# Pooled attention with a gated MLP: the decoding, splitting and copying of the first two batches on other engines, a left-over V tile of its own, a new order

## The chip, the core and the metric

The kernel runs on one core of a Trainium2 chip. The metric is the device time of one execution in microseconds (us); the median of three runs is given with the lowest and the highest. Engines: TensorE (PE, with its weight loads PEld), VectorE (DVE), ScalarE (ACT), GpSimd (POOL), and SyncE (SP), which issues nearly all DMAs from one queue, in order.

## The reference

Eight batches, eight heads, 576 positions of 64. Keys and values are averaged over groups of 8 positions (72 remain), attention over these, then a gated MLP with a spatial gate:

```python
k_p = k.reshape(B, H, Sp, pool, D).mean(axis=3)          # Sp = 72
v_p = v.reshape(B, H, Sp, pool, D).mean(axis=3)
attn = softmax(q @ k_p.T / sqrt(D))                      # 576 x 72 a head
x = (attn @ v_p), heads side by side                     # 8 x 576 x 512
h = gelu_tanh(x @ w_in)                                  # 512 -> 1024
u, v = h[..., :512], h[..., 512:]
v_n = (v - mean(v)) / sqrt(var(v) + 1e-6) * g_ln
v_s = einsum('ts,bsd->btd', w_sg, v_n) + b_sg            # 576 x 576
out = x + (u * v_s) @ w_out                              # 512 -> 512
```

`w_in` and `w_out` come as 64-bit floats, all else as 32-bit floats.

## The kernel before

The large products are taken in fp32r, as three matmuls each: an operand is split into a high part (a cast by ScalarE) and a low part (value minus high part, as a rule by GpSimd), and high*high, high*low and low*high are summed in PSUM.

The work is cut into steps, each a Python generator that issues its instructions stage by stage (a `yield` ends a stage). A step has a letter, a number and a batch:

- A, B: load of the keys and the values (`kvraw`, halves 0 and 1). E: load of what is left over, the groups beyond 128 rows of two heads (`left`). C: load of q (four pairs of heads g).
- K0, K1, P0, P1: pooling of keys and values: on TensorE for batches 0 and 1 (16 rows of matmuls against `ident`, a copy out of PSUM), on VectorE later. K2: pooling of the left-over part (`lp`, VectorE), transposes, and the scaled keys `kbd`. P2: the values as weights: `vb` (or `vbh`, `vbl`), and `vl` for the left-over ones.
- Q: q transposed (`qT`). S0 to S3: scores of a pair of heads, their maximum (`nmax`, VectorE), ten exponentials with sums (ScalarE), normalising (`e`, VectorE), the left-over columns (`el`, GpSimd).
- T0 to T3: e transposed (`ah`, low part `al`), through TensorE in batch 0, through DRAM (`tfar`) later. L: the same for the left-over columns (`lt`, `lfar`).
- V0 to V3: attention times values, then `x32` and its high and low part `xhl`, and for the last 64 positions both parts packed (`xta`).
- H0 to H4: x times the v half of w_in by blocks of positions, Gelu, normalising, `vhh` and `vhl`. U0 to U3: the u half, Gelu. W0 to W3: the spatial product, gate, `ghi` and `glo`. O0 to O3: times w_out, plus x. Z: transposing and storing.
- Weights, once: l.. loads, and v0 to v3, u0 to u3, o0 to o3 decode a quarter of the 64-bit weights: a first step on ScalarE (L1340), three on VectorE (L1342 to L1344), two on ScalarE (L1347, L1348), three on GpSimd (L1350 a product, m; L1351 a subtraction, d; L1352 a sum, a) that give `wil` or `wol`. s0 to s4 transpose and split w_sg.

What sets the order is a table written out by hand, `PROLOGUE` and then `PERIOD` for batch after batch: an entry `S1+0` advances step S1 of batch 0 by one stage; entries for batches that don't exist emit nothing. Each engine gets its instructions in the order of the table and keeps it; semaphores do the rest. PSUM has two tiles each for `mps` (H, U, W, most of O, the scores of batch 0, the decoding of v) and for `aps` (everything of the attention), taken in turn.

In batch 0 (`WHOLE`) the left-over values are written by step P2 over a part of the tile `left` (`v32`), and V reads them from there. Step E of batch 1 loads into the same buffer.

Of the kernel before, what the change touches and what calls it, by code (L numbers as in the profile page):

```python
# [8 lines left out]
F32 = mybir.dt.float32  # L9
# [14 lines left out]
lv0 A1+0 E0+0 K1+0 A0+0 v1 v1 K0+0 v0 v0 K1+0 K2+0 C0+0 Q0+0 K0+0 K2+0 K2+0 Q0+0 S0+0 C1+0 S0+0 S0+0 Q1+0 Q1+0 S1+0  # L24
C2+0 S1+0 Q2+0 S1+0 Q2+0 S0+0 S2+0 C3+0 Q3+0 v0 S1+0 S2+0 Q3+0 T0+0 v1 A0+1 B0+0 S2+0 S3+0 S3+0 A1+1 ls0 B1+0 K1+1
T0+0 S0+0 S3+0 P1+0 S1+0 K1+1 P0+0 lv1 K0+1 S2+0 v0 S3+0 v2 v2 v1 v3 v3 S3+0 P2+0 s1 v2 C0+1 S2+0 v2 s1 K0+1 L0+0 L0+0
s3 v3 lu0 T1+0 V0+0 Q0+1 s3 s1 s3 u0 u0 s2 T1+0 V1+0 lo0 V0+0 u0 s4 o0 V1+0 T2+0 o0 T2+0 T3+0 V2+0 s2 lu1 v3 u1 T3+0
V3+0 u0 V2+0 u2 s2 u1 u1 u2 s4 V3+0 B0+1 B1+1 E0+1 s0 K2+1 C1+1 P1+1 s0 P1+1 P0+1 K2+1 P0+1 K2+1 S0+1 u1 V1+0 V2+0 u2
u3 s4 V0+0 o0 o1 Q1+1 S1+1 s0 S0+1 u3 S1+1 S0+1 S1+1 V1+0 S0+1 V3+0 H0+0 C2+1 Q2+1 H2+0 S1+1 S2+1 V2+0 S2+1 C3+1 Q3+1
S3+1 o1 H0+0 lo1 H2+0 P2+1 C1+2 V3+0 V0+0 u3 S2+1 u2 H4+0 S0+1 o0 H0+0 u3 P2+1 U3+0 H2+0 o2 S3+1 H4+0 T0+1 S3+1 S2+1  # L30
o2 H4+0 o2 o1 S1+1 U3+0 S3+1 S2+1 H0+0 S3+1 o2 T0+1 U0+0 C0+2 L0+1 H4+0 H0+0 H0+0 T1+1 H4+0 o1 L0+1 U0+0 H1+0 P2+1
T0+1 H2+0 L0+1 H3+0 A0+2 P2+1 T0+1 H1+0 H2+0 L0+1 E0+2 V0+1 T1+1 T1+1 Q0+2 H2+0 U2+0 H1+0 Q1+2 H4+0 T2+1 K0+2 T1+1
V1+1 T2+1 H3+0 H3+0 L0+1 H1+0 U1+0 U2+0 H3+0 H4+0 H1+0 T2+1 H3+0 H1+0 A1+2 H3+0 T3+1 H4+0 V0+1 W1+0 V1+1 T2+1 V2+1
# [1159 lines left out]
def tile_pooled_attn_gmlp(ctx: ExitStack, tc: tile.TileContext, q, k, v, w_in, g_ln, w_sg, b_sg, w_out, out):  # L1193
# [96 lines left out]
    gcol = const.tile([P, DF2 // P], F32, name="gcol")  # L1290

    st = {}

    def load(o, i, queue=nc.sync):
        queue.dma_start(o, i)  # L1295

# [219 lines left out]
    def step_P(b, i):  # L1516
# [18 lines left out]
        for h in range(2):  # L1535
            nc.scalar.mul((vb[b] if b in WHOLE else vbh)[:, :, D * h:D * h + D], vp, head[:, h:h + 1])  # L1536
# [388 lines left out]
```

## Time and profile before

| | |
|---|---|
| median of 3 runs | 593.61 us (593.04 to 594.01) |
| the profiled execution: its time, its span | 592.2 us, 590.5 us |
| mean granted clock of TensorE | 0.984 |
| busy in the span: PE, PEld, DVE, ACT, POOL | 548.3, 510.5, 444.5, 357.8, 240.1 us |
| share of PE in the span | 93% |
| share in the chain that ended last: PE, DVE, ACT, DMA, SP's queue | 62%, 9%, 8%, 8%, 4% |
| HBM read and written | 49.73 and 20.94 MB |

Busy time of TensorE is the union of its matmuls' modelled times, so a busy TensorE need not be one at its peak. In rows of waits the first name is what waited, the name behind the arrow what ended the wait. Line numbers are those of the kernel before; all matmuls are issued by one helper at L1237, so groups are told apart by their tiles.

### The profile page before, as it was taken

How to read it: one execution, taken by the hardware profiler on the slowest of the kernel's cores; microseconds unless marked ns; L12 is line 12 of the kernel's file. 1: busy time of each engine (PE TensorE's matmuls, PEld its weight loads, DVE VectorE, ACT ScalarE, POOL GpSimd, SP SyncE). 2: the span in 40 equal slices, each digit the busy share in tenths (PEclk: the TensorE clock that was granted, in tenths of full speed). 3: DMA queues.
4: the chain of work that ended last, by engine and by line, in shares of the span. 5: the costliest groups of instructions: out<-in, count | busy, mean ns of one | idle time of the engine just before them, and what ended most of it. 6: DMA issues, size and time to landing. Idle time of an engine off the chain costs nothing.

```text
span 590.5 us, 10655 instructions
## 1 busy us (share of the span) xinstructions
PE 548.3 (93%) x3664; PEld 510.5 (86%) x3664; DVE 444.5 (75%) x610; ACT 357.8 (61%) x1115; POOL 240.1 (41%) x272
## 2 busy tenths in 40 slices
PE   4699777999999999999999999999999999999992
PEld 4576666988899999999899989999999989989992
DVE  4587898979888879978697988689767878546242
ACT  2897895477736974487737875498347884433110
POOL 2286858345342622370424434441425233434030
PEclk9999888999999999999999999999999999999996
DMA  9991535454569346554767276706755422310215
GB/s 239 333 296 29 122 79 141 127 142 86 138 171 178 76 98 184 123 108 120 164 141 161 71 159 150 153 3 148 170 131 110 97 68 66 85 23 1 41 22 81
DMA packets 191607, 71.39 MB, mean 121 GB/s; under 512 B 152576, under 2 KB 175488, under 8 KB 191552
## 3 DMA queue, kind: packets, MB, share of 16 engines
q1 hardware_dynamic: 186784, 70.11, 49.5%
q10 hardware_dynamic: 4768, 0.59, 0.7%
q8 instruction: 29, 0.48, 0.3%
q14 instruction: 26, 0.21, 0.1%
HBM read 49.73 MB, written 20.94 MB: 120 GB/s over the span
## 4 chain that ended last, share of the span: by engine, by line
PE 62%; DVE 9%; ACT 8%; DMA 8%; SPq 4%; issue 2%; POOL 1%; ACTq 0%; DVEq 0%; POOLq 0%
PE mps L1237 50%; PE aps L1237 11%; ACT e L1601 4%; SPq L1295 4%; DMA out<-y 2%; DMA al<-tfar 2%; DMA y<-lfar 1%; DMA kvraw<-in_v 1%; ACT L1601 1%; DMA left<-in_v 1%; DVE al L1674 1%; DMA lfar<-y 1%; DVE kp L1455 1%; DVE vp L1455 1%; DVE lp L1455 1%
## 5 line engine op out<-in xcount | busy, mean ns | idle before, releaser
L1237 PE MATMUL mps<-xhl,wih 128*128 128x288 f32 x512 | 89.9, 298 | 0.0
L1601 ACT ACTIVATE e<-aps,nmax 128x72 f32<-128x72 f32 x280 | 85.5, 352 | 6.7 <-DVE nmax L1584 6.5
L1237 PE MATMUL mps<-wih,xhl 128*128 128x512 f32 x256 | 85.1, 399 | 0.6 <-ACT u L1783 0.6
L1237 PEld LDWEIGHTS mps<-xhl,wih 128*128 128x128 f32 x512 | 77.2, 190 | 1.4 <-ACT vg L1745 0.2
L1808 POOL TENSOR_TENSOR glo<-u,ghi 128x576 fp32r<-128x576 f32 x32 | 45.9, 1446 | 71.3 <-ACT ghi L1806 71.2
L1601 ACT ACTIVATION_READ_ACCUMULATOR e<-aps,nmax 128x1 f32 x280 | 66.6, 238 | 0.0
L1766 POOL TENSOR_TENSOR vhl<-vg,vhh 128x512 fp32r<-128x512 f32 x32 | 46.6, 1461 | 39.6 <-ACT vhh L1764 34.9
L1712 POOL TENSOR_TENSOR xhl<-x,xhl 128x576 fp32r<-128x576 f32 x32 | 45.7, 1443 | 37.1 <-ACT xhl L1710 37.1
L1237 PEld LDWEIGHTS mps<-wih,xhl 128*128 128x128 f32 x256 | 48.2, 188 | 12.3 <-ACT u L1783 1.2
L1237 PE MATMUL mps<-xhl,wil 128*128 128x288 f32 x256 | 55.3, 298 | 1.8 <-POOL wil L1352 1.8
L1237 PE MATMUL mps<-wsh,vhl 128*128 128x288 f32 x256 | 55.1, 296 | 0.3 <-POOL vhl L1766 0.3
L1237 PE MATMUL mps<-wsh,vhh 128*128 128x288 f32 x256 | 55.3, 297 | 0.0
L1671 ACT CAST ah<-al 128x640 fp32r<-128x640 f32 x28 | 20.5, 730 | 57.4 <-DMA al<-tfar 47.7
L1237 PE MATMUL mps<-wsl,vhh 128*128 128x288 f32 x256 | 54.7, 295 | 0.0
L1237 PE MATMUL mps<-ghi,woh 128*128 128x288 f32 x240 | 52.3, 299 | 0.0
L1237 PE MATMUL mps<-glo,woh 128*128 128x288 f32 x240 | 51.5, 296 | 0.0
L1237 PE MATMUL mps<-ghi,wol 128*128 128x288 f32 x240 | 51.4, 295 | 0.0
L1237 PE MATMUL mps<-wil,xhl 128*128 128x512 f32 x128 | 50.6, 395 | 0.0
L1752 POOL TENSOR_TENSOR rstd<-mv,eps 128x1 f32<-128x1 f32 (+1 forms) x40 | 12.3, 309 | 93.4 <-DVE mv L1750 87.8
L1237 PE MATMUL aps<-kbd,qT 128*128 128x144 f32 x280 | 41.3, 302 | 6.1 <-DVE qT L1567 3.2
L1237 PEld LDWEIGHTS aps<-kbd,qT 128*128 128x128 f32 x280 | 38.3, 201 | 7.8 <-ACT vbh L1536 3.4
L1237 PEld LDWEIGHTS mps<-xhl,wil 128*128 128x128 f32 x256 | 41.8, 190 | 2.0 <-POOL wil L1352 2.0
(162 smaller groups left out, 1402.5 us busy)
## 6 DMA issues: line engine op xcount, KB each, us to landing
tfar<-y SPq DMA_DIRECT2D x28, 320.0 KB, 2.4
al<-tfar SPq DMA_DIRECT2D x112, 80.0 KB, 2.2
out<-y SPq DMA_DIRECT2D x118, 72.0 KB, 2.1
kvraw<-in_k SPq DMA_DIRECT2D x16, 512.0 KB, 4.3
kvraw<-in_v SPq DMA_DIRECT2D x16, 512.0 KB, 4.6
qraw<-in_q SPq DMA_DIRECT2D x112, 72.0 KB, 2.6
raw<-in_moe_w_in SPq DMA_DIRECT2D x4, 1024.0 KB, 8.5
y<-lfar SPq DMA_DIRECT2D x42, 80.0 KB, 2.2
```

What stands on the lines that cost most here:

```text
L1237: nc.tensor.matmul(o, lhsT, rhs, start=start, stop=stop)
L1295: queue.dma_start(o, i)
L1455: nc.vector.tensor_reduce(out=o, in_=t.rearrange("p a (r d) -> p a d r", r=POOL), axis=AX.X, op=ALU.add)
L1601: nc.scalar.activation(e[:, i, h], slots[i][:, h], AF.Exp, bias=nmax[:, i, h:h + 1], **acc)
L1671: nc.scalar.copy(ah, al)
L1674: nc.vector.tensor_tensor(lo, al, ah.bitcast(F32), op=ALU.subtract)
L1712: nc.gpsimd.tensor_tensor(xhl[:, 1, g], x32, xhl[:, 0, g].bitcast(F32), op=ALU.subtract)
L1752: nc.gpsimd.tensor_tensor(rstd, mv[:, 1:2], eps[:n, 1:2], op=ALU.add)
L1766: (nc.gpsimd if i < NT - 1 else nc.vector).tensor_tensor(lo, vg, hi.bitcast(F32), op=ALU.subtract)
L1808: nc.gpsimd.tensor_tensor(glo[:, d], uf, ghi[:, d].bitcast(F32), op=ALU.subtract)
```

## The change

- Two helpers choose the engine by a key: `copy` (ScalarE, or VectorE if the key is in the table `OTHER`) and `combine` (GpSimd, or VectorE if it is there). The keys name step, batch and part: `H12` is the low part of H2 of batch 1, `o3m` and `o3d` the product and the subtraction of o3.
- From GpSimd to VectorE go nine low parts (H1 of batch 0, H2 and H3 of batch 1, V3 of batch 0, V1 of batch 1, W1 of batch 0, W1 to W3 of batch 1) and ten instructions of the decoding (o0d o1d o3m o3d u1d v0m v1m v1a v3m v3d). For V, H and W the key's batch is at most 2, and no key has a 2, so later batches stay as they were.
- From ScalarE to VectorE go three copies out of PSUM (K0 of batch 1, T0 of batch 0, s2); Q0 of batch 0 goes the other way.
- In batch 0 the high part of x is cast straight from PSUM, ahead of the copy to `x32`, instead of from `x32`.
- In batch 0 the left-over V gets a tile of its own, `vl`.
- The table is new: one `PROLOGUE` for all batches and an empty `PERIOD`. It advances the same steps by the same stages. In the first two batches many stand elsewhere, from batch 2 on mostly neighbours change places.

```diff
+OTHER = """
+H01 H12 H13 K10 Q01 Q02 Q03 T00 V03 V11 W01 W11 W12 W13 o0d o1d o3d o3m s2 u1d v0m v1a v1m v3d v3m
+""".split()
...
+    def copy(o, i, key):
+        if key in OTHER:
+            nc.vector.tensor_copy(o, i)
+        else:
+            nc.scalar.copy(o, i)
+
+    def combine(o, x, y, op, key):
+        (nc.vector if key in OTHER else nc.gpsimd).tensor_tensor(o, x, y, op=op)
...
-            nc.gpsimd.tensor_tensor(low32, x, low32, op=ALU.mult)
-            nc.gpsimd.tensor_tensor(top, top, hi.bitcast(F32), op=ALU.subtract)
-            nc.gpsimd.tensor_tensor(lo, low32, top, op=ALU.add)
+            combine(low32, x, low32, ALU.mult, f"{name}{c}m")
+            combine(top, top, hi.bitcast(F32), ALU.subtract, f"{name}{c}d")
+            combine(lo, low32, top, ALU.add, f"{name}{c}a")
...
-                nc.scalar.copy(kp, ps)
+                copy(kp, ps, f"K{b}{i}")
...
         v32 = st.pop(("left", b))[64:96, :, 0:4 * D].rearrange("p g (a d) -> p g a d", a=4)
+        if b in WHOLE:
+            v32 = per.tile([96, 2, 4, D], F32, name="vl")[64:96]
...
         if b in WHOLE:
-            nc.scalar.copy(x32.rearrange("p (a n) -> p a n", a=2), ps[:, :, 0:HALF])
+            xs, hi = ps[:, :, 0:HALF], xhl[:, 0, g].rearrange("p (a n) -> p a n", a=2)
+            copy(hi, xs, f"h{b}{g}")
+            copy(x32.rearrange("p (a n) -> p a n", a=2), xs, f"x{b}{g}")
...
-        nc.gpsimd.tensor_tensor(xhl[:, 1, g], x32, xhl[:, 0, g].bitcast(F32), op=ALU.subtract)
+        combine(xhl[:, 1, g], x32, xhl[:, 0, g].bitcast(F32), ALU.subtract, f"V{min(b, 2)}{g}")
...
-        (nc.gpsimd if i < NT - 1 else nc.vector).tensor_tensor(lo, vg, hi.bitcast(F32), op=ALU.subtract)
+        if i < NT - 1:
+            combine(lo, vg, hi.bitcast(F32), ALU.subtract, f"H{min(b, 2)}{i}")
...
-        nc.gpsimd.tensor_tensor(glo[:, d], uf, ghi[:, d].bitcast(F32), op=ALU.subtract)
+        combine(glo[:, d], uf, ghi[:, d].bitcast(F32), ALU.subtract, f"W{min(b, 2)}{d}")
```

The pooling copies of P, the transposed q, `ah` and `lt` of batch 0 and `wsh` go through `copy` in the same way.

Three places of the new order. First TensorE, between V3 of batch 0 and H0 of batch 0. Before (the last row of V3, s0, the pooling of the values of batch 1, K2 with keys and left-over part, the scores S0 and S1 of batch 1, H0):

```order
L1237 MATMUL aps<-lt,left 128x288
L1374 MATMUL mps<-ident,stage 128x128 x4
L1374 MATMUL mps<-ident,stage 128x64
L1237 MATMUL aps<-kvraw,ident 128x128 x16
L1503 MATMUL aps<-ident,kp 64x128 x4
L1504 MATMUL aps<-ident,lp 128x128
L1237 MATMUL aps<-kbd,qT 128x144 x10
L1237 MATMUL mps<-wih,xhl 128x512
```

After (s3, K2, V3, S0 and S1, H0; the line numbers are those of the changed kernel, 137 the helper of all matmuls):

```order
L283 MATMUL mps<-ident,stage 128x128 x4
L283 MATMUL mps<-ident,stage 128x64
L414 MATMUL aps<-ident,kp 64x128 x4
L415 MATMUL aps<-ident,lp 128x128
L137 MATMUL aps<-ah,vb 128x288
L137 MATMUL aps<-lt,vl 128x288
...
L137 MATMUL aps<-kbd,qT 128x144 x10
L137 MATMUL mps<-wih,xhl 128x512
```

K2 now stands ahead of V3, and the pooling of the values is gone from here; it stands behind H2.

Second SP's queue, around the load of batch 1's left-over part. Before (weights, the values of batch 1, the left-over part, three loads of q of four DMAs each):

```order
L1295 DMA raw<-in_moe_w_in 128x4x512
L1295 DMA kvraw<-in_v 128x2x512 x2
L1295 DMA left<-in_k 32x1x512 x2
L1295 DMA left<-in_v 32x1x512 x2
L1295 DMA qraw<-in_q 32x18x32 x12
L1295 DMA raw<-in_moe_w_out 128x4x512
```

After:

```order
L204 DMA raw<-in_moe_w_out 128x4x512
L204 DMA left<-in_k 32x1x512 x2
L204 DMA left<-in_v 32x1x512 x2
L204 DMA qraw<-in_q 32x18x32 x4
L204 DMA raw<-in_moe_w_in 128x4x512
L204 DMA qraw<-in_q 32x18x32 x4
L204 DMA kvraw<-in_v 128x2x512
```

The left-over part moved ahead of the last load of w_in; two of the three loads of q behind it, C0 and C1, are issued earlier still, and only one half of the values stands behind it.

Third ScalarE, between the exponentials of S1 and the later two sets of batch 1. Before (exponentials of S0 and S1, xta, Gelu of H0 and H2, vbh, xta, u3, exponentials of S2):

```order
L1601 ACTIVATE e,ssum<-aps,nmax 128x72 x20
L1714 CAST xta<-xhl 128x128 x2
L1745 ACT_TABLE_LOAD
L1745 ACTIVATE vg<-mps 128x512 x2
L1536 ACTIVATE vbh<-vp,head 128x4x64 x2
L1714 CAST xta<-xhl 128x128 x2
L1347 ACTIVATE raw<-raw 128x4x128
L1348 CAST wih<-top 128x4x128
L1601 ACT_TABLE_LOAD
L1601 ACTIVATE e,ssum<-aps,nmax 128x72 x10
```

After, from the two copies of the pooled values on (ahead of them stand u1, one xta, the Gelu of H0 and u2), up to the exponentials of S3 and S2:

```order
L198 COPY vp<-aps 128x128 x2
L629 CAST xta<-xhl 128x128 x2
L449 ACTIVATE vbh<-vp,head 128x4x64 x2
L249 ACTIVATE top<-raw 128x512
L660 ACTIVATE vg<-mps 128x512
L654 COPY vg<-mps 64x512
L256 ACTIVATE raw<-raw 128x4x128
L257 CAST wih<-top 128x4x128
L463 CAST vl<-left 32x512 x3
L514 ACT_TABLE_LOAD
L514 ACTIVATE e,ssum<-aps,nmax 128x72 x20
```

More of the decoding, the copies of P and the casts of `vl` now stand between the two pairs of sets; the Gelu of U1 follows behind the second pair.

More of the change, by code (lines that the diff above doesn't have):

```diff
@@ L29 @@
[L29 to L33, printed above, removed]
@@ new lines @@
+Z0+0 S2+2 P2+2 S3+2 Z2+0 S2+2 H1+1 S3+2 H0+1 H1+1 Z0+0 H0+1 V3+1 H2+1 L0+2 O3+0 T0+2 T1+2 L0+2 A1+3 P2+2 P2+2 H0+1
+H2+1 O3+0 P2+2 H1+1 T0+2 O3+0 L0+2 L0+2 H0+1 H1+1 H3+1 H0+1 H1+1 A0+3 H2+1 V0+2 Q0+3 E0+3 K0+3 T1+2 C2+3 H3+1 V0+1
+U0+1 H0+1 U0+1 T2+2 V2+1 U3+1 C1+3 L0+2 T1+2 T1+2 U3+1 H2+1 K2+3 V1+2 H4+1 U2+1 Z1+0 Z3+0 H2+1 H2+1 H4+1 H4+1 H4+1
+H3+1 H4+1 H3+1 T2+2 Z1+0 H4+1 U1+1 T2+2 T2+2 H3+1 U2+1 H3+1 H4+1 B0+3 V0+2 H4+1 Z3+0 W1+1 T3+2 U1+1 V2+2 W0+1 K1+3
+V1+2 K2+3 T3+2 Q1+3 V1+2 V2+2 W1+1 T3+2 W2+1 K2+3 P0+3 T3+2 V3+2 B1+3 K2+3 V3+2 V2+2 C3+3 W0+1 W2+1 S0+3 V3+2 Q2+3
@@ new lines @@
+S0+3 S1+3 P1+3 W3+1 W1+1 V0+2 W0+1 S0+3 A0+4 S1+3 W3+1 W2+1 C0+4 Q3+3 V2+2 S1+3 S0+3 H2+2 W0+1 H2+2 P2+3 W2+1 W1+1
+U2+2 H2+2 V3+2 S3+3 S1+3 V0+2 S0+3 W3+1 O0+1 W3+1 S3+3 U2+2 S2+3 T0+3 S3+3 P2+3 O0+1 T1+3 S2+3 O1+1 O1+1 V1+2 P2+3
+O0+1 S1+3 S3+3 T0+3 O2+1 S2+3 S3+3 O2+1 O1+1 H1+2 Z1+1 T0+3 P2+3 H2+2 Z1+1 O2+1 O3+1 S2+3 O3+1 H1+2 S2+3 L0+3 Z2+1
+Z2+1 H2+2 H0+2 H1+2 O3+1 L0+3 H2+2 H0+2 K0+4 C1+4 H4+2 A1+4 L0+3 Q0+4 H4+2 T0+3 H0+2 U3+2 H4+2 L0+3 U3+2 T3+3 V0+3
+H3+2 H1+2 H1+2 T1+3 H4+2 H1+2 H3+2 E0+4 U1+2 T1+3 L0+3 U1+2 H4+2 U0+2 T2+3 H0+2 H4+2 H4+2 B0+4 Z0+1 Q1+4 T1+3 H0+2
@@ new lines @@
+H3+2 Z3+1 H0+2 H3+2 H4+2 K2+4 V1+3 T2+3 Z0+1 H3+2 V0+3 U0+2 H3+2 W0+2 T2+3 W2+2 K1+4 Z3+1 V1+3 W0+2 T2+3 V2+3 K2+4
+T3+3 W2+2 W1+2 V2+3 P0+4 W3+2 K2+4 W0+2 T3+3 W1+2 C3+4 T3+3 V3+3 W0+2 W1+2 B1+4 W2+2 V1+3 W2+2 K2+4 C2+4 V3+3 W3+2
+S0+4 W3+2 S0+4 S1+4 P1+4 W1+2 S0+4 W3+2 O0+2 Q3+4 P2+4 V3+3 V2+3 C1+5 V0+3 O1+2 O0+2 S0+4 S1+4 O0+2 O1+2 T0+4 S3+4
+V2+3 O1+2 S3+4 A0+5 H1+3 S0+4 O2+2 P2+4 S1+4 S1+4 V1+3 H1+3 S3+4 Q2+4 S2+4 O2+2 K0+5 S2+4 T0+4 O3+2 B0+5 S2+4 C0+5
+H1+3 O2+2 V3+3 S1+4 O3+2 H2+3 H1+3 T1+4 Z2+2 O3+2 S3+4 T0+4 Z2+2 S2+4 H0+3 P2+4 H2+3 S2+4 V0+3 U3+3 S3+4 L0+4 L0+4
@@ L1376, in step_s @@
         if c < NT - 1:
-            yield from split(wsh[:, c], wsl[:, c], ps[:, 0:S], nc.vector)
+            copy(wsh[:, c], ps[:, 0:S], f"s{c}")
+            yield
+            nc.vector.tensor_tensor(wsl[:, c], ps[:, 0:S], wsh[:, c].bitcast(F32), op=ALU.subtract)
         else:
@@ L1525, in step_P @@
                 yield
-                nc.scalar.copy(vp, ps)
+                copy(vp, ps, f"P{b}{i}")
             elif b in BY_PE:
@@ L1563, in step_Q @@
             yield
-            nc.vector.tensor_copy(qT, ps[:, 0:S])
+            copy(qT, ps[:, 0:S], f"Q{b}{g}")
             st["qT", b, g] = qT
@@ L1635, in step_L @@
                 lt = st["lt", b, gp] = per.tile([96, S], F32, name="lt", tag=f"lt{gp}")
-                nc.scalar.copy(lt[64:96], ps[32 * gp:32 * gp + 32, 0:S])
+                copy(lt[64:96], ps[32 * gp:32 * gp + 32, 0:S], f"L{b}{gp}")
             return
@@ L1659, in step_T @@
             ah = per.tile([P, S], F32, name="ah")
-            nc.scalar.copy(ah, ps[:, 0:S])
+            copy(ah, ps[:, 0:S], f"T{b}{g}")
             st["a", b, g] = ah, None
@@ L1709, in step_V @@
             nc.scalar.copy(x32[:, 4 * P:S].rearrange("p (q j) -> p q j", q=2), o[:, 2:4, P:BAND])
-        nc.scalar.copy(xhl[:, 0, g], x32)
+            nc.scalar.copy(xhl[:, 0, g], x32)
         yield
-        nc.gpsimd.tensor_tensor(xhl[:, 1, g], x32, xhl[:, 0, g].bitcast(F32), op=ALU.subtract)
+        combine(xhl[:, 1, g], x32, xhl[:, 0, g].bitcast(F32), ALU.subtract, f"V{min(b, 2)}{g}")
         yield
@@ L1765, in step_H @@
         yield
[L1766 removed]
+        if i < NT - 1:
+            combine(lo, vg, hi.bitcast(F32), ALU.subtract, f"H{min(b, 2)}{i}")
+        else:
+            nc.vector.tensor_tensor(lo, vg, hi.bitcast(F32), op=ALU.subtract)
     def halves(ps, pairs, first, last):
```

1200 lines of the change are left out of this document (42 added, 1158 removed).

## The prediction, made before the changed kernel was run

> **What bounds the kernel now.** I read the busy times by stretch first (they say in which stage TensorE still has idle time), then the waits of TensorE before 150 us, then the timeline around each of these waits, last the chain that ended last. All times are us from the start of the profiled execution (span 590.5, its own time 592.2; the median of the runs is 593.61, so 1.4 above). Columns of the stretches: length, then busy time and count of PE, weight loads, DVE, ACT, POOL, then clock, DMA share, GB/s.
>
> ```profile
> 7.56:54.00 46.44, 39.43 (x239) 29.87 (x239) 34.84 (x47) 34.16 (x123) 21.88 (x21) 1.00 0.79 236
> 54.00:101.00 47.00, 35.79 (x196) 31.07 (x196) 39.38 (x53) 38.58 (x129) 38.30 (x35) 0.92 0.47 112
> 101.00:142.00 41.00, 38.09 (x271) 36.85 (x270) 35.66 (x44) 23.55 (x75) 20.64 (x18) 0.97 0.48 117
> 142.00:510.00 368.00, 366.21 (x2495) 347.13 (x2494) 300.26 (x422) 241.03 (x752) 132.72 (x155) 1.00 0.53 123
> ```
>
> From 142 on TensorE is idle for 368.00 - 366.21 = 1.8 us in 368: there it is the bound, and whatever is saved before 142 reaches the end whole. Before, idle time is 7.0, 11.2 and 2.9 us. So the change is worth what it does to the time at which TensorE gets through the first two batches, above all between 54 and 101. The waits there, largest first (total, times, longest):
>
> ```profile
> PE aps L1237 <- DVE lt L1651: 3.3, 1, 3.3
> PE aps L1237 <- DVE qT L1567: 3.2, 1, 3.2
> PE mps L1237 <- POOL wil L1352: 1.8, 1, 1.8
> PE aps L1504 <- DVE lp L1455: 1.4, 1, 1.4
> PE aps L1237 <- DVE e L1612: 1.4, 1, 1.4
> ```
>
> Each long wait is also followed by a stretch at half the clock:
>
> ```profile
> 62.65:66.06 3.41, 3.41 (x16) 3.41 (x15) 2.44 (x3) 3.40 (x10) 3.25 (x4) 0.50 0.73 117
> 76.30:79.72 3.42, 3.42 (x13) 3.02 (x14) 3.32 (x8) 3.39 (x10) 0.97 (x2) 0.50 0.38 62
> 100.20:103.61 3.41, 3.41 (x16) 3.41 (x15) 3.38 (x7) 0.00 (x0) 1.22 (x3) 0.50 0.28 76
> ```
>
> A wait thus costs its idle time and up to 3.41 / 2 = 1.7 us more.
>
> **The left-over tile and the order up to H0 of batch 0.** Before, the keys and values left over of batch 1 could be fetched only when V3 of batch 0 had read its V tile out of the same buffer (start, duration; the first row is the queue, the next two the chain, the rest PE):
>
> ```profile
> 54.10 1.24 SPq L1295 DMA_DIRECT2D left<-in_k  x2
> 56.02 2.29 DMA left<-in_v
> 58.44 1.93 DVE lp L1455
> 54.75 3.84 PE L1237 MATMUL aps<-kvraw,ident 128*128 128x128 f32 x32
> 60.41 0.33 PE L1504 MATMUL aps<-ident,lp 128*128 128x128 f32 x1 [1.39 <-DVE lp L1455]
> 61.68 4.27 PE L1237 MATMUL aps<-kbd,qT 128*128 128x144 f32 x20 [0.93 <-ACT kbd L1510]
> 65.58 0.71 PE L1237 MATMUL mps<-wih,xhl 128*128 128x512 f32 x1
> ```
>
> With a tile of its own the fetch stands ahead of the last q loads and has no such wait, lp is reduced ahead of V3, K2 stands ahead of V3 and the 3.84 us of value pooling (P0, P1) go behind H2. I let V3 end at 55 (54 before; K2 now stands in front of it, and T2 and T3 no longer follow each other ahead of V1). Then come the 20 score matmuls, 4.27 at most: H0 starts at about 59.3, 6.3 earlier; after giving back P0 and P1 TensorE is 2.5 ahead. This is not yet a gain, because the next thing late is ScalarE.
>
> **ScalarE up to the last exponentials of batch 1.** V0 of batch 1 waits for lt, lt for the left-over columns of all four softmaxes, these for the exponentials. First and last of them before, one set of ten with its accumulator reads, the load of a table, and what ScalarE did between:
>
> ```profile
> 65.28 0.32 ACT L1601 ACTIVATE e<-aps,nmax 128x72 f32<-128x72 f32 x1
> 85.60 0.37 ACT L1601 ACTIVATE e<-aps,nmax 128x72 f32<-128x72 f32 x1
> 69.13 3.13 ACT e L1601 x20
> 72.67 1.28 ACT L1745
> 65.28:85.97 20.69, 15.71 (x78) 13.23 (x78) 19.01 (x30) 19.86 (x95) 14.40 (x16) 0.90 0.31 90
> L1550 ACT CAST vl<-left 32x512 fp32r<-32x512 f32 x21 | 13.0, 618 | 0.4
> L1347 ACT ACTIVATE raw<-raw 128x512 f32<-128x512 uint32 x12 | 8.4, 697 | 0.1
> L1348 ACT CAST wih<-top 128x512 fp32r<-128x512 f32 x8 | 5.0, 623 | 0.0
> ```
>
> ScalarE was full: 19.86 of 20.69. After the change the scores are there at about 58.5, and with DVE's maximum and the u2 start ahead the first exponential comes at about 60.1, 5.2 earlier. But the new order puts more in front of the last one. Of the 19.86, o2's first step and one xta (some 1.0) go behind it; three pairs of L1347 and L1348 (u1, u2, u3) stand there instead of one, 2 x 1.3 = 2.6 more, and two vp copies (some 0.6), u3's first step (0.7, as L1347) and three vl casts, 3 x 0.62 = 1.9. That is 24.7 from 60.1, and u1's and u3's pairs each wait for three DVE steps of 1.9 in all, of which about half shows each time (1.8): the last exponential ends at 86.6 instead of 85.97, **+0.6**. What was won ahead of H0 is spent here.
>
> **From the exponentials to lt.** Here POOL's work doubled DVE's. The first two rows are the same kind of instruction beside a POOL instruction and alone, the next two stand on the way to lt, then the two transfers on it:
>
> ```profile
> 42.27 1.64 DVE L1343 SCALAR_TENSOR_TENSOR top<-raw,top 128x512 int32<-128x512 int32 x1
> 51.50 0.69 DVE L1343 SCALAR_TENSOR_TENSOR top<-raw,top 128x512 int32<-128x512 int32 x1
> 94.44 3.27 DVE L1674 TENSOR_TENSOR al<-al,ah 128x640 fp32r<-128x640 f32 x1 [0.33 <-ACT ah L1671]
> 97.73 1.79 DVE L1651 TENSOR_TENSOR lt<-y,lt 32x640 fp32r<-32x640 f32 x1
> 105.29 0.84 DVE al L1674
> 88.81 1.79 DMA lfar<-y
> 91.51 2.05 DMA y<-lfar
> ```
>
> Alone, al takes 0.84; beside POOL's o1 it took 3.27, and lt 1.79. After: from 86.6 DVE normalises S2 (1.3), does o2's three steps (2.0) and transposes el (0.5): 91.0 (88.8 before). Until lt stand T1 0.8, al 0.84, the lp of batch 2 1.9, one moved o1 subtraction 0.7, statistics and scaling of H1, H2, H4 2.5 and lt 0.84: 7.6, so lt ends at 98.6; the transfers, 1.79 + 2.05 and two issues, end at about 95.5 and are hidden. Before, lt ended at 99.5: **-0.9**. DVE's work here is as long as without the moves; it is only no longer doubled, since o1 and o2 now find POOL with less behind it.
>
> The other waits: Q2 and Q3 of batch 1 stood late on DVE (3.2); they now stand ahead of H0's statistics, and U1 instead of U3 is the first U, with its wil ready at about 72 (1.8 before). Both costs vanish, but both lie ahead of V0, where TensorE waits for lt anyway: 0. A new wait takes their place: U3 needs the PSUM tile of U1, whose Gelu stands behind the exponentials and a table load, at about 89. TensorE is then idle for some 5 us, between H1 and U3.
>
> **The half clock.** The stretch at 100.20 to 103.61 followed the wait for lt and fell on work that bounds: four of U2's matmuls took 1.16 in it and 0.69 behind it.
>
> ```profile
> 100.88 1.16 PE L1237 MATMUL mps<-xhl,wih 128*128 128x288 f32 x4
> 103.69 0.69 PE L1237 MATMUL mps<-xhl,wih 128*128 128x288 f32 x4
> ```
>
> With the long wait now ahead of U3, the half clock falls on U3, ahead of the wait for lt, which hides it. Bounds 0 and -1.7; I take **-1.5**, since I have lt within 1 us of U0's end. The Trainium skill, "TensorE: Matmul & The Clock Gate", Part 1, has an idle window of about 3.4 us halve the clock and one busy window restore it. Here waits of 3.2 and 3.3 us did it, in stretches of 3.41: the trace agrees. By that rule the half clock would return behind V0 only if lt came some 3 us after U0.
>
> **From W1 to O.** V3 of batch 1 waited 0.79 for ah, and 0.24 more for al; W3 (28 matmuls, some 3.7 us) now stands between, so **-1.0**. S2 of batch 2 waited 1.4 for e of an earlier set; it now stands ahead of O1. I take half, **-0.7**, because DVE is fuller there.
>
> ```profile
> 120.21 0.39 PE L1237 MATMUL aps<-ah,vbh 128*128 128x256 f32 x1 [0.79 <-ACT ah L1671]
> L1350 POOL TENSOR_TENSOR raw<-raw 128x512 f32<-128x512 f32 x12 | 12.9, 1079 | 15.8 <-DVE raw L1344 11.2 <-ACT raw L1347 3.8 <-issue 0.7
> L1808 POOL TENSOR_TENSOR glo<-u,ghi 128x576 fp32r<-128x576 f32 x4 | 5.6, 1430 | 1.3 <-ACT ghi L1806 1.3
> L1766 DVE TENSOR_TENSOR vht<-vg,vht 64x512 fp32r<-64x512 f32 x8 | 6.7, 839 | 7.5 <-ACT vht L1764 7.4
> ```
>
> The moves by themselves: 19 subtractions, products and sums leave POOL (1.1 to 1.4 each, some 24 us) for DVE, where the nearest rows are 0.69 and 0.84 (some 14 us); three copies go from ScalarE to DVE and one back. Five of the 19 fall between 101 and 142 (H1, V1, o3 twice, W1): 3.8 us, where DVE had 41.00 - 35.66 = 5.3 idle. That fits only just. Bounds 0 and +2.5 (all of it on the path, less what the shorter stretch needs anyway); I take 0, since the pooling and q transposes there can wait until after 142, where DVE is busy 300 of 368.
>
> Reading xhl's high part straight from PSUM: the cast comes one copy earlier, the tile is freed no earlier: 0, covered by the POOL queue behind it. From batch 2 on the order differs by neighbours that change places, and no instruction moves to another engine: 0, with 0.6 either way for the 1.8 us of waits there. Table entries for batches that don't exist emit nothing: 0.
>
> Sum: -0.9 - 1.5 - 1.0 - 0.7 = **-4.1**. 592.2 - 4.1 = 588.1 for such an execution; on the median 593.61 - 4.1 = **589.5**. A measurement of this kernel can tell 0.2%, 1.2 us, from nothing.
>
> **Rivals.** *More is won.* I let ScalarE stand still some 6 us between 24 and 60, waiting for maxima, decoding and T2. If DVE, relieved, is ahead there, the last exponentials end 4 us earlier, and lt and U1's Gelu with them: -8.1, 585.5. For it: ScalarE was busy 34.16 of 46.44 from 7.56 to 54. Against: DVE had 34.84 there and gets more.
>
> *It is given back.* The 3.8 us on DVE from 101 to 142 land on the path behind W1 (o3's two moved steps stand ahead of W2's scaling): +2.5 to +3.5 on the sum, 592.5 to 593.5, no change.
>
> *Slower: the exponentials of batch 1 come late.* The place is ScalarE ahead of S3's set: u1's and u3's pairs wait there for three DVE steps each, in order, with S3, S2 and U1's Gelu behind them. If POOL doubles DVE there as at 42.27 (1.64 for 0.69), u2, u1, o1 and u3 cost up to 4 x 1.9 = 7.6 more; lt follows one for one. The sum is eaten once the last exponential ends at 90.7 instead of 86.6; at the full price it is +3.5, 597. For it: DVE was busy 19.01 of 20.69 there. Against: POOL has three moved instructions, some 4 us, less to do there. The Trainium skill, "SBUF — State Buffer", "Who interferes with whom", speaks for it: a DVE instruction with two SBUF inputs and a GpSimd one that reads SBUF exclude each other, and the later waits out the whole of the other. The row at 94.44 agrees (3.27 - 0.84 = 2.43, about two POOL instructions), and the moved ones have two SBUF inputs.
>
> **How the numbers follow.** Forecast (-1.2 to -6.5) 0.55, more 0.15, given back 0.15, slower 0.15: faster 0.70, same 0.15, slower 0.15. The range reaches to the second case's 585.0 and to the top of the third, 594.8; beyond lie half of the second case and most of the fourth.
>
> **What would show it.** Right: H0 of batch 0 starts near 59; ScalarE has next to no idle time from 60 to 87; the largest wait of TensorE is U3's, for u of U1; no half clock behind V0 of batch 1; lt ends near 98.5; V3's wait is gone. Wrong: the last exponential ends before 84 or after 90; DVE subtractions of 1.6 and more between 60 and 76; or new waits of TensorE on DVE between 101 and 142.

## The result, and the profile after

The changed kernel takes 576.95 us (575.42 to 578.14), the kernel before on the same chip 593.81 (593.04 to 594.31): 0.9716 of it, interval 0.969 to 0.9741. A second set of runs (e13 below) gave 0.9729 (0.9708 to 0.9751). The mean of the two, 0.9723 or 16.5 us less, is what the experiments below are held against. The prediction had 589.5 and 585.0 to 594.8: faster was right, the size was a quarter of what came.

The profiled execution takes 577.16 (span 575.4, 15.1 less than before). Its stretches, with the columns as before (length, then busy time and count of PE, weight loads, DVE, ACT, POOL, then clock, DMA share, GB/s):

```profile
7.56:54.00 46.44, 41.49 (x263) 32.49 (x264) 39.14 (x55) 36.80 (x130) 20.52 (x18) 1.00 0.95 259
54.00:101.00 47.00, 38.53 (x234) 34.22 (x233) 44.80 (x70) 39.44 (x129) 30.37 (x32) 0.96 0.48 131
101.00:142.00 41.00, 40.26 (x274) 37.92 (x272) 37.49 (x57) 30.78 (x117) 15.68 (x16) 1.00 0.45 102
142.00:510.00 368.00, 364.65 (x2504) 346.66 (x2503) 298.00 (x411) 233.64 (x713) 132.11 (x150) 1.00 0.52 121
```

TensorE's idle time in the first three is 5.0, 8.5 and 0.7 us (7.0, 11.2 and 2.9 before). VectorE now does 125 instructions between 7.56 and 101, where it did 100. The waits of TensorE between 54 and 142:

```profile
PE mps L137 <- ACT u L701: 4.6, 1, 4.6
...
PE mps L137 <- POOL glo L201: 0.7, 1, 0.7
PE aps L137 <- DVE lt L564: 0.5, 1, 0.5
```

The places that the prediction gave times for, in the timeline after: H0 of batch 0, first and last exponential of batch 1, the first lt, and U3 with what stands behind it.

```profile
54.52 0.49 PE L137 MATMUL mps<-wih,xhl 128*128 128x512 f32 x1
55.33 0.31 ACT L514 ACTIVATE e<-aps,nmax 128x72 f32<-128x72 f32 x1
79.63 0.44 ACT L514 ACTIVATE e<-aps,nmax 128x72 f32<-128x72 f32 x1
90.65 0.81 DVE L564 TENSOR_TENSOR lt<-y,lt 32x640 fp32r<-32x640 f32 x1
82.72 1.33 PE L137 MATMUL mps<-xhl,wih 128*128 128x288 f32 x4 [4.61 <-ACT u L701]
87.40 0.69 PE L137 MATMUL mps<-xhl,wih 128*128 128x288 f32 x4
```

H0 starts 11.1 earlier than before, the last exponentials end 5.9 earlier (80.07), lt 8.1 earlier. TensorE is 12.2 ahead when O0 of batch 0 ends (133.49 against 145.69) and 10.4 ahead at the last matmul (568.64 against 579.06). The other 4.7 of the 15.1 lie behind the last matmul, where the prediction had not looked. There, from before, the transposes into y and the store queue of ScalarE:

```profile
572.71 0.78 DVE L1857 STREAM_TRANSPOSE y<-x 128x576 f32<-128x576 f32 x1
576.72 10.89 ACTq L1295 DMA_DIRECT2D out<-y  x10
582.68 0.78 DVE L1857 STREAM_TRANSPOSE y<-x 128x576 f32<-128x576 f32 x1 [5.35 <-DMA out<-y]
```

and from after:

```profile
562.29 0.78 DVE L775 STREAM_TRANSPOSE y<-x 128x576 f32<-128x576 f32 x1
563.10 9.55 ACTq L204 DMA_DIRECT2D out<-y  x10
566.95 0.78 DVE L775 STREAM_TRANSPOSE y<-x 128x576 f32<-128x576 f32 x1
570.23 0.48 DVE L746 STREAM_TRANSPOSE y<-x 128x288 f32<-128x288 f32 x1 [1.10 <-DMA out<-y]
```

Before, Z1's y of the last batch was finished at 573.49, but the order had its store behind Z0's, which began at 576.72. There are two buffers of y, so the third transpose waited 5.35 for a store that had been let go more than 3 us late. After, the store begins right behind its transpose (563.07, 563.10), and that wait is gone; one of 1.10 is left, at the fourth.

### The profile page after: what moved, and what is told of

It is laid out like the page before. It is cut to its first block, busy times and chain, and to the rows that moved or that the text cites. A ratio compares the mean times of both kernels' runs of the same rounds, so it can differ in the third digit from the quotient of the medians.

```text
span 575.4 us, 10670 instructions
## 1 busy us (share of the span) xinstructions
PE 543.8 (95%) x3664; PEld 507.2 (88%) x3664; DVE 447.2 (78%) x631; ACT 355.3 (62%) x1111; POOL 217.5 (38%) x253
## 4 chain that ended last, share of the span: by engine, by line
PE 65%; DVE 12%; ACT 11%; DMA 5%; issue 3%; POOL 2%; SPq 1%; DVEq 0%; ACTq 0%; POOLq 0%
PE mps L137 52%; PE aps L137 12%; ACT e L514 5%; DMA al<-tfar 2%; SPq L204 1%; POOL glo L201 1%; DVE e L525 1%; ACT L514 1%; DMA kvraw<-in_k 1%; DVE nmax L497 1%; DVE al L587 1%; DVE ssum L521 1%; DVE bst L664 1%; DVE top L252 1%; PE mps L283 1%
## 5 line engine op out<-in xcount | busy, mean ns | idle before, releaser
L201 POOL TENSOR_TENSOR glo<-u,ghi 128x576 fp32r<-128x576 f32 x28 | 41.2, 1486 | 70.0 <-ACT ghi L724 70.0
L201 POOL TENSOR_TENSOR xhl<-x,xhl 128x576 fp32r<-128x576 f32 x30 | 43.5, 1459 | 36.9 <-ACT xhl L625 36.3
L201 POOL TENSOR_TENSOR vhl<-vg,vhh 128x512 fp32r<-128x512 f32 x29 | 39.5, 1365 | 45.9 <-ACT vhh L679 45.4
L715 DVE SCALAR_TENSOR_TENSOR mps<-mps,gcol,bbc 128x576 f32<-128x576 f32 x32 | 26.3, 822 | 27.4 <-PE mps L137 27.3
L670 DVE SCALAR_TENSOR_TENSOR vg<-vg,mv,rstd 128x512 f32<-128x512 f32 (+1 forms) x40 | 37.1, 942 | 7.0 <-POOL rstd L668 6.6
```

What stands on the lines that cost most here:

```text
L201: (nc.vector if key in OTHER else nc.gpsimd).tensor_tensor(o, x, y, op=op)
L670: nc.vector.scalar_tensor_tensor(vg, vg, mv[:, 0:1], rstd.broadcast_to([n, DF2]), op0=ALU.subtract, op1=ALU.mult)
L715: nc.vector.scalar_tensor_tensor(vs, vs, gcol[:, d:d + 1], bbc.rearrange("p (a n) -> p a n", a=2), op0=ALU.mult, op1=ALU.add)
```

## The experiments

Ratios are to the kernel before on the same chip. A ratio's interval is 0.0015 to 0.0042 to either side (0.9 to 2.5 us), so differences below 2 us between two runs are not read as such.

**The end alone (e1).** One entry of the old order moves; all else is the kernel before.

```diff
-... O1+7 Z1+7      O2+7 O0+7 O0+7 O2+7 Z0+7 O3+7 O3+7 O2+7 Z0+7 Z1+7 Z2+7 ...
+... O1+7 Z1+7 Z1+7 O2+7 O0+7 O0+7 O2+7 Z0+7 O3+7 O3+7 O2+7 Z0+7      Z2+7 ...
```

> The kernel before with one entry of the order moved: the store of Z1 of the last batch stands ahead of the store of Z0 instead of behind it. Theory (the ring of y): before, 11.4 us pass between the last matmul and the end, since Z1's y lies finished at 573.5 while its store is queued behind Z0's (issued at 576.7 and 577.6), and the third y has to wait 5.35 us for that buffer; after, 6.8 us pass. So this one entry is worth -4.6, to about 589.0, with the wait of Z2's y down from 5.35 to under 1. Rival (the last 14 stores are bound by what they move, in whatever order they are issued): within 1 us of before, the wait only goes elsewhere. Nothing moves ahead of the last matmul by either.

590.01 us, 0.9929 (0.9909 to 0.9949): -4.2. The timeline of the end in this run:

```profile
575.08 0.78 DVE L770 STREAM_TRANSPOSE y<-x 128x576 f32<-128x576 f32 x1
575.89 9.55 ACTq L201 DMA_DIRECT2D out<-y  x10
579.74 0.78 DVE L770 STREAM_TRANSPOSE y<-x 128x576 f32<-128x576 f32 x1
583.02 0.48 DVE L741 STREAM_TRANSPOSE y<-x 128x288 f32<-128x288 f32 x1 [1.09 <-DMA out<-y]
```

The third transpose no longer waits, and the queue moves the same ten transfers in the same 9.55 as after. That the stores are bound by what they move is out; a quarter of the gain is this one entry.

**The tile of its own alone (e2).**

```diff
+        if b in WHOLE:
+            v32 = per.tile([96, 2, 4, D], F32, name="vl")[64:96]
```

> The kernel before, with a tile of its own for the left-over V of batch 0 and nothing else. Theory (this part only allows the new order): lp of batch 1 comes up to 1.4 earlier, as the wait of 1.39 for it goes; ScalarE was full from 65 to 86, so at most these 1.4 reach the end: -0.5 to -1.5, 592.1 to 593.1. Rival (the buffer alone was what held the scores of batch 1, and with them lt and V0 of batch 1): -4 or more, 589.5 or less.

593.78 us, 0.9992 (0.9978 to 1.0007): nothing that can be measured. In its profile H0 of batch 0 starts 1.8 earlier (63.75), and lt ends where it did (99.44 against 99.52). The tile only allows an order in which K2 of batch 1 stands ahead of V3.

**The new engines in the old order (e3), the new order with the old engines (e4).** For e3 the table of keys is the new one and the order the old one, without the tile; for e4 the order and the tile are new, and

```diff
-OTHER = "H01 H12 H13 K10 Q01 Q02 Q03 T00 V03 V11 W01 W11 W12 W13 o0d o1d o3d o3m s2 u1d v0m v1a v1m v3d v3m"
+OTHER = "Q00 Q01 Q02 Q03"
-            copy(hi, xs, f"h{b}{g}")
             copy(x32.rearrange("p (a n) -> p a n", a=2), xs, f"x{b}{g}")
+            copy(hi, x32.rearrange("p (a n) -> p a n", a=2), f"h{b}{g}")
```

> The kernel before in its old order, with the instructions shared out as in the changed kernel (19 from GpSimd to VectorE, three copies from ScalarE to VectorE, one back, the high part of x cast from PSUM), without the tile of its own. Theory (the order carries the gain): within 2 us of before, 591.5 to 595.5, since the instructions change engine without the waits of TensorE on lt, qT and wil changing their place. Rival (relieving GpSimd is what brings forward DVE, whose instructions beside GpSimd's took 1.64 instead of 0.69): V0 of batch 0 ends 2 or more earlier than 42.3 and lt of batch 1 4 or more earlier than 99.5, 589.5 or less.

> The changed kernel with every instruction on its old engine and the high part of x cast from x32 again: the new order and the tile of its own alone. Theory (the order carries the gain, the end of the program with it): at most 3 us behind the changed kernel, 577 to 580. Rival (the moves carry the 10 us that do not come from the end): 584 or more, with lt of batch 1 at 97 or later instead of 91.5.

e3: 614.59 us, 1.0361 (1.0324 to 1.0397), 21 slower: both expectations fell. e4: 584.68, 0.9844 (0.9822 to 0.9867), 9.3 faster: the rival, 7.2 behind the changed kernel. So the same moves of engines cost 21 in the old order and bring 7.2 in the new one. In the old order they stand at the wrong places of VectorE's queue. Waits of e3 from 36 to 60, first TensorE's, then VectorE's, and a row of V1 of batch 0:

```profile
PE mps L280 <- DVE top L249: 2.9, 2, 2.6
PE aps L174 <- DVE kp L193: 0.9, 1, 0.9
...
DVE top L248 <- ACT top L246: 9.5, 1, 9.5
...
50.74 1.33 PE L134 MATMUL aps<-ah,vb 128*128 128x288 f32 x2
```

TensorE waits for VectorE's decoding and for a copy queued behind it, and runs at half the clock for 17.07 us from 41.97 on, which is worth up to 8.5 (two matmuls of V1 take 1.33, where 0.75 and less is usual). ScalarE's first step of o0 takes the buffer of lt, which V1 reads until 55.84, and starts at 55.92; VectorE, in order, waits 9.5 for it. (That V1's reading released it follows from the kernel's buffers and the two times; the profile names no releaser there.) Each queue holds up the next. And e4 is nearly what the prediction described (first and last exponential, lt):

```profile
58.92 0.30 ACT L511 ACTIVATE e<-aps,nmax 128x72 f32<-128x72 f32 x1
85.83 0.43 ACT L511 ACTIVATE e<-aps,nmax 128x72 f32<-128x72 f32 x1
96.70 0.81 DVE L561 TENSOR_TENSOR lt<-y,lt 32x640 fp32r<-32x640 f32 x1
```

**One group of moves taken back (e5 to e9).** Each is the changed kernel with keys left out of the table, or with the cast put back:

```diff
 e5: -o0d o1d o3d o3m u1d v0m v1a v1m v3d v3m
 e6: -H01 H12 H13 V03 V11 W01 W11 W12 W13
 e7: -K10 T00 s2  +Q00
 e8: the high part cast from x32
 e9: e6 and e8 together
```

> The changed kernel with the ten instructions of the decoding (v0m v0.. v1a v1m v3d v3m o0d o1d o3d o3m u1d) back on GpSimd; all else as changed. All the moves together are worth some 7.5 us in the new order. Theory (the decoding carries it: GpSimd needs 1.1 to 1.4 us where VectorE needs 0.7, and the low parts of x and of H queue behind it): 4 to 5 later than the changed kernel, 581 to 582. Rival (the copies out of PSUM carry it, as they keep TensorE's tiles): at most 1.5 later, 578.5.

> The changed kernel with the nine low parts (of H1, V3 and W1 of batch 0, of H2, H3, V1, W1, W2 and W3 of batch 1) back on GpSimd. Theory (a share of the 7.5 us of the moves, from H on): 1.5 to 2.5 later than the changed kernel, 578.5 to 579.5, with GpSimd's glo later for O1 of batch 0, where TensorE waited 0.70 for it. Rival (GpSimd has room for them once the decoding has left it): within 0.7 of the changed kernel.

> The changed kernel with the four copies out of PSUM where they were: K0 of batch 1, T0 of batch 0 and s2 on ScalarE, the transposed q of Q0 on VectorE. Theory (the decoding carries the gain of the moves): at most 1.5 later, 578.5. Rival (the copies carry it: with all moves undone S0 of batch 0 waited 1.56 for qT instead of 0.94 for kbd, and S3 of batch 0 ran at half the clock): 3 or more later, 580 or more, with V0 of batch 0 at 41 or later instead of 38.5.

> The changed kernel with the high part of x of batch 0 cast from x32, behind the copy, as before. Theory (costs nothing, as the prediction had it): within 0.5 of the changed kernel. Rival (the low part and H0 wait for the cast, and it takes part in the 7.5 us): 1 or more later, 578 or more.

> The changed kernel with both the nine low parts back on GpSimd and the high part of x of batch 0 cast from x32. Each alone gave 578.8, 1.9 more than the changed kernel, but with runs from 576.4 to 581.7, and in the profiles neither has a later TensorE but for the start and one stretch at half the clock behind a late load. Theory (both are worth next to nothing, and the moves' 7.5 us are the decoding and the copies): within 1.2 of the changed kernel, below 578.2. Rival (they add up): 579.5 or more.

e5: 580.39 us, 0.9777 (0.9747 to 0.9807), 3.2 behind the changed kernel's 0.9723. e6: 578.84, 0.9763 (0.9721 to 0.9805). e7: 578.08, 0.974 (0.9712 to 0.9768). e8: 578.86, 0.9744 (0.9711 to 0.9776). e9: 579.46, 0.9742 (0.9719 to 0.9766). Only e5 can be told from the changed kernel; for e6 to e9 it stays open whether they cost nothing or up to 2 us, and e9, with two groups taken back, shows no more than either. What the decoding does on GpSimd is seen in e5 where VectorE decodes o1 (three steps), with GpSimd's rows of the same time behind them:

```profile
64.57 1.50 DVE L248 TENSOR_SCALAR top<-top 128x512 int32<-128x512 int32 x1
66.10 1.68 DVE L249 SCALAR_TENSOR_TENSOR top<-raw,top 128x512 int32<-128x512 int32 x1
67.82 1.41 DVE L250 SCALAR_TENSOR_TENSOR raw<-top 128x512 int32<-128x512 int32 x1
...
64.52 1.27 POOL L198 TENSOR_TENSOR top<-top,wih 128x512 f32<-128x512 f32 x1
65.87 1.37 POOL L198 TENSOR_TENSOR wil<-raw,top 128x512 fp32r<-128x512 f32 x1
```

and in the changed kernel, where the subtraction of u1 is VectorE's (last row):

```profile
63.95 0.42 DVE L251 TENSOR_SCALAR top<-top 128x512 int32<-128x512 int32 x1
64.41 0.69 DVE L252 SCALAR_TENSOR_TENSOR top<-raw,top 128x512 int32<-128x512 int32 x1
65.13 0.71 DVE L253 SCALAR_TENSOR_TENSOR raw<-top 128x512 int32<-128x512 int32 x1
65.74 0.69 DVE L201 TENSOR_TENSOR top<-top,wih 128x512 f32<-128x512 f32 x1
```

4.59 for three steps beside GpSimd, 2.51 for the three and the moved one without it: VectorE is 2.1 earlier with more work. The transposed q of S3 stands behind these steps, and TensorE waits 1.14 for it in e5 and not at all after. Over all of VectorE's instructions up to 142 us that both executions have, those of e5 take 6.2 longer, while the ten moved ones take 6.9 in the changed kernel (0.69 each). So VectorE has about as much to do either way; what counts is which of its instructions get shorter.

**The decoding alone (e10, e11).** e10 is e3 without the ten decoding keys; e11 is e4 with them and nothing else moved.

> The kernel before in its old order with the low parts and the copies shared out anew and the high part of x cast from PSUM, but the decoding on GpSimd as before. With the decoding too it took 614.6, 20.5 more than before. Theory (the moved decoding steps stand at places of the old order where VectorE has to wait for ScalarE or GpSimd in the midst of a quarter, and all of VectorE's queue waits with them): 597 or less. Rival (the copies out of PSUM, now queued behind VectorE's decoding, hold TensorE's tiles: kp was waited for 0.93): 606 or more.

> The new order and the tile of its own, with the old engines but for the ten decoding instructions on VectorE. Without these ten it took 584.7; taking them back from the changed kernel cost 3.4. Theory (a product or a subtraction on VectorE costs 0.69 and spares the others on VectorE the 0.7 to 1.0 each by which they are longer beside GpSimd's): 2.5 to 4.5 less than 584.7, 580.2 to 582.2, with the mean of VectorE's instructions between 54 and 101 below 0.70 us (0.74 without them, 0.64 in the changed kernel). Rival (they only pay together with the copies): within 1 of 584.7.

e10: 601.97 us, 1.0118 (1.0095 to 1.0141), between the two expectations: of the 21 that the moves cost in the old order some 14 are the decoding's, 7 the others'. e11: 581.15, 0.9763 (0.9735 to 0.979), as the theory had it: 4.8 less than e4 (3.2 by taking it back). VectorE between 54 and 101, in e4 and in e11:

```profile
54.00:101.00 47.00, 44.35 (x60) 0.96 0.46 122
...
54.00:101.00 47.00, 44.42 (x69) 0.93 0.48 138
```

Nine instructions more in the same busy time, 0.64 each instead of 0.74. The last exponential of batch 1 ends at 82.27 in e11 and lt at 93.61 (86.26 and 97.51 in e4): the moved decoding alone brings lt 3.9 earlier.

**Two edits at the two ends (e12).** A try to go below the changed kernel:

```diff
-lv0 A1+0 K1+0 v1 A0+0 v0 E0+0 K0+0 v0 K1+0 C0+0 K2+0 ...
+A1+0 A0+0 E0+0 lv0 K1+0 v1 v0 K0+0 K1+0 C0+0 K2+0 v0 ...
-            y = ring(per, [P, S // 32, 32], "y", 2)
+            y = per.tile([P, S // 32, 32], F32, name="y", tag="qraw0")
```

> The changed kernel with two more edits, one at each end: the first weight load stands behind the loads of keys and left-over part of batch 0 (with the first decoding step of VectorE behind K2's reduction), and the y of the last block of output has a buffer that was used for q and is free by then. Theory: TensorE starts 0.5 to 1.5 earlier than 7.33, and the wait of 1.10 for an output store goes; 574.0 to 575.5. Rival (the start is paid back by the decoding, which comes later, and the last store ends as late as before): within 0.8 of the changed kernel.

580.35 us, 0.9756 (0.9736 to 0.9776), about 2 behind the changed kernel: the rival, and worse. TensorE's and ScalarE's first waits, and S0 of batch 0:

```profile
PE aps L134 <- DMA kvraw<-in_k: 4.9, 1, 4.9
...
ACT mps L246 <- DMA raw<-in_moe_w_in: 8.7, 1, 8.7
...
16.48 2.77 PE L134 MATMUL mps<-kbd,qT 128*128 128x144 f32 x10 [0.94 <-ACT kbd L418]
```

TensorE starts 2.4 earlier (7.3 after), but ScalarE's first decoding step stands ahead of the copies of the pooled keys and waits for the weights that now come later. The scores of S0 start 1.5 later than after (15.00), and at half the clock. At the end the wait of 1.10 for y is gone, and the span still ends 6.7 behind the last matmul (6.8 after).

**Why the decoding gains on VectorE (e13 to e15).** e13 is the changed kernel again. e14 adds to it eight useless instructions on GpSimd, e15 sixteen, of about the same total time; GpSimd's sum overwrites what they write.

```diff
+            for part in "md":
+                if f"{name}{c}{part}" in OTHER and f"{name}{c}a" not in OTHER:
+                    nc.gpsimd.tensor_tensor(lo, x, x, op=ALU.mult)      # e14
+                    for _ in range(2): nc.gpsimd.memset(lo.bitcast(F32), 0.0)   # e15
             combine(low32, x, low32, ALU.mult, f"{name}{c}m")
```

> The changed kernel itself, unaltered, as the measure for the two runs beside it and for the small differences of the earlier ones. It gave 0.9716 of before; its runs were 575.4 to 578.1. Expected: 0.970 to 0.975.

> The changed kernel (its moved decoding stays on VectorE), with eight useless products on GpSimd added, at the places where eight of the ten moved instructions stood: each reads SBUF and writes a part of wil or wol that GpSimd's sum overwrites next. So GpSimd is as full as with the decoding on it. Theory (what the moved decoding is worth is that VectorE's instructions with two SBUF inputs are no longer drawn out beside GpSimd's): 2.5 to 5 more than the changed kernel, with VectorE's three steps of o1 taking 3 to 4.6 instead of 1.8. Rival (GpSimd's own lateness is what costs): 2.5 to 5 more too, and the same as the next run; so the two runs are read together.

> As the run before, but in place of each product two fills of the same part of wil or wol with zero (0.57 each by the fills at the start of the program), which occupy GpSimd for about as long and read nothing. Theory (VectorE is drawn out by GpSimd's reads of SBUF): within 1.2 of the changed kernel, with VectorE's steps of o1 at 1.8 to 2.2. Rival (GpSimd's lateness costs): 2.5 to 5 more than the changed kernel, like the run before.

e13: 578.15 us, 0.9729. e14: 582.98, 0.9795 (0.9773 to 0.9817). e15: 578.08, 0.9723 (0.9702 to 0.9744). GpSimd's added groups, e14 and then e15:

```profile
L258 POOL TENSOR_TENSOR wol<-raw 128x512 fp32r<-128x512 f32 x4 | 4.9, 1234 | 5.8 <-DVE raw L250 5.7
L258 POOL TENSOR_TENSOR wil<-raw 128x512 fp32r<-128x512 f32 x4 | 4.2, 1040 | 8.4 <-DVE raw L250 5.2 <-DVE ssum L521 3.1
...
L259 POOL MEMSET wil<- 128x512 f32 x8 | 4.5, 565 | 0.3
L259 POOL MEMSET wol<- 128x512 f32 x8 | 4.2, 525 | 0.3
```

With 9.1 us of GpSimd's time that read SBUF the kernel takes 3.9 more (0.9795 against 0.9729); with 8.7 us that only write, no more. The six runs of e14 (580.5 to 583.85) all lie above the five of e15 (576.65 to 579.32). The two runs alone don't tell reads from lateness, though. A product has to wait for VectorE's `raw` (GpSimd was idle for 14.2 ahead of the eight), a memset for hardly anything (0.6), so the memsets could fill time in which GpSimd was idle anyway. The trace has to decide. Here is the place where o3 is decoded, in e14 (the products, then VectorE's product and subtraction of o3) and in e13:

```profile
124.32 2.49 POOL L258 TENSOR_TENSOR wol<-raw 128x512 fp32r<-128x512 f32 x2 [5.72 <-DVE raw L250]
124.35 1.57 DVE L198 TENSOR_TENSOR raw<-raw 128x512 f32<-128x512 f32 x1
125.84 1.52 DVE L198 TENSOR_TENSOR top<-top,woh 128x512 f32<-128x512 f32 x1
...
119.23 0.69 DVE L198 TENSOR_TENSOR raw<-raw 128x512 f32<-128x512 f32 x1
119.84 0.68 DVE L198 TENSOR_TENSOR top<-top,woh 128x512 f32<-128x512 f32 x1
```

Beside the products VectorE's two instructions take more than twice as long. GpSimd's sum behind them then waits 0.69 for VectorE, so GpSimd is not what is late here. TensorE was 5.2 behind e13 when V0 of batch 1 started (98.31 against 93.12) and is 6.9 behind when O1 of batch 0 starts (129.55 against 122.66): 1.7 of this reach TensorE. The Trainium skill, "SBUF — State Buffer", "Who interferes with whom", has just this: a VectorE instruction with two SBUF inputs contends with a GpSimd one that reads SBUF, not with one that only writes it. These rows agree, and so do the two such steps of v3 in e15, which start beside memsets (41.91 and 42.64) and take 0.69 each. Two more instructions of VectorE are drawn out in e14 (1.23 and 1.20 at 45.17 and 69.25, instead of 0.41 and 0.42), but these are TENSOR_SCALAR with one input, of which that sentence says nothing.

Not all of the 3.9 is shown to be the price of the reads. The profiled execution of e14 has a span 6.5 longer than that of e13, and TensorE was 2.5 behind at 43.47 (41.02 in e13), when only one of the eight products had run, and 3.6 behind at V1's first matmul (46.09 against 42.46). Up to there it had waited for a later load of w_sg (0.73 instead of 0.44) and run at half the clock from 39.99 to 46.82, which e13 did not. So some 2.9 of the 6.5 are left for the products. All six runs of e14 have a lower granted clock (0.983 to 0.989) than the nine of e13 and e15 (0.990 to 0.995); whether the products bring this about stays open. One number of e14's expectation missed: o1's three steps took 2.6 there and not 3 to 4.6.

## Why the prediction was right or wrong

- *The new order, -4.1.* e4 less the end (-9.3 and -4.2) leaves -5.1, with some 1.8 either way. For a kernel whose engines had not changed the path was right, and its steps fit that run: first exponential at 60.1 (58.92 measured), last one ending at 86.6 (86.26), lt at 98.6 (97.51). The sizes of the terms were not right. lt ended 2.0 earlier than before, where 0.9 was forecast. Of the 3.2 forecast behind it (half clock, V3, S2) TensorE gained only 1.0 in the profiled executions: V0 of batch 1 starts at 97.57 instead of 99.58, the last matmul ends at 576.02 instead of 579.06. O1 of batch 0 had new waits there, 1.3 for glo and 0.8 for ghi. That the sum comes near -5.1 is in part luck. Two sums do not close, either: 86.6 with 1.3, 2.0 and 0.5 gives 90.4 and not 91.0, so by its own terms lt would have ended at 98.0 and the sum been -4.7; and +2.5 to +3.5 on 589.5 gives 592.0 to 593.0, not 592.5 to 593.5.
- *"The moves by themselves: ... I take 0".* This is the step that failed: -7.2 (e4 against the changed kernel), of which 3.2 to 4.8 is the decoding. The step counted what VectorE takes over (0.69 each) and left out what GpSimd no longer does to the instructions beside it, though its own two rows had the size of it: 1.64 beside GpSimd and 0.69 alone. Measured, the ten moved instructions brought VectorE 6.9 and freed 6.2 of it (e5), so its sum hardly changed; the gain is that the freed time lies on the way to qT of S3 and the exponentials, where VectorE was 2.1 earlier. With all the moves ScalarE's first exponential came at 55.33 and the last ended at 80.07, 6.5 earlier than forecast, and lt at 91.46, 7.1 earlier. The bounds, 0 to +2.5, left out a gain without a reason. By what way the other moves bring their 2.4 to 4.0 stays open.
- *From batch 2 on "neighbours change places ... 0, with 0.6 either way".* The second failed step: -4.2 in the last batch alone (e1). The price was looked for in the waits of TensorE (1.8 us there), and the end lies behind TensorE's last instruction.
- *The half clock, V3's wait, U3's wait.* Right: 4.61 ahead of U3 (some 5 forecast), four of U3's matmuls at 1.33 and later ones at 0.69, none at half the clock behind V0 of batch 1, V3 without a wait.
- *DVE between 101 and 142, 0.* Right: it does 57 instructions instead of 44 there, and TensorE has no wait on it there; 0.7 on GpSimd's glo is new.
- *The rivals.* "More is won" had the right direction and gave it 0.15 and 4 us; the last exponentials ended 6.5 earlier. Its place was right in part only: of ScalarE's idle time between 24 and 60, 5.8 before, 3.9 is left, and VectorE was not relieved but fuller (39.14 instead of 34.84 busy from 7.56 to 54). The fourth rival named the right mechanism, VectorE drawn out by GpSimd, with the wrong sign: the three steps of o1, which it had grow, took 1.82 with the moves, and 4.59 with the decoding left on GpSimd (e5). Of the signs set down as "wrong if", the first came true: the last exponential ended before 84.

What each part is worth, from the runs: the end -4.2, the order -5.1, the moved decoding -3.2 to -4.8, the other moves and the cast the rest of -16.5, 2.4 to 4.0, which no run of one group tells from nothing. The tile of its own: nothing alone.

## What to carry to other kernels

Cost a move between GpSimd and VectorE on both sides: what the instruction takes on the new engine, and what its reads of SBUF no longer add to the instructions beside it. Here the two nearly cancelled on VectorE (6.9 and 6.2), and the gain lay in which instructions got shorter. Such a move has no price of its own, though: the same moves cost 21 us in one order and brought 7 in another, since each queue runs in order and a misplaced instruction holds all behind it. And look at the time behind the last matmul as a stage of its own: with two buffers, a finished store that is queued behind an unfinished one cost 4 us.

## What was not expected of the hardware

The half clock does not need a long wait of TensorE. In the kernel before, the stretch from 62.65 on stood behind waits of 1.39 and 0.93. In e8 (first three rows) and e13 (last two) TensorE was idle for 0.45 and 0.44 us between 36.00 and 39.70, for the load of w_sg, after 8 us without a gap. Behind it, e8 ran 3.4 us at half the clock, e13 none (columns: length, busy time and count of PE, clock, DMA share, GB/s):

```profile
28.00:36.00 8.00, 8.00 (x74) 1.00 0.96 324
36.00:39.70 3.70, 3.25 (x12) 0.98 1.06 337
39.70:43.10 3.40, 3.40 (x15) 0.52 1.04 386
...
36.00:39.70 3.70, 3.26 (x11) 1.00 1.06 373
39.70:43.10 3.40, 3.40 (x24) 1.00 1.07 374
```

The prediction's reading, that waits of 3.2 and 3.3 us brought the half clock, does not cover this stretch of e8; what decides between the two executions is not shown. A stretch of 3.4 us is worth up to 1.7, more than half the spread of one kernel's runs here (575.4 to 578.1), and e14 had one of 6.83 at the same place. So a difference of that size between two profiled executions is read from several runs, not from two traces.
